# Float64 weights to float32: the low word rounded to three bits and added as an integer, with a shorter schedule of steps

## Chip, cores and metric

One core of one Trainium2 chip. The metric is device time in microseconds from start to end of one execution; it is the median over several runs. Profiles come from one further execution, which the hardware profiler recorded.

## What is computed

Three layers follow one another: an attention with 32 global and 512 local tokens per sequence (4 sequences, 8 heads of 64), where a local token sees the global ones and a window of 32 to either side; an FFN with squared ReLU; and an FFN whose activation is a rational function.

```python
a_l = sm(concat(s_lg, where(|i - j| <= 32, s_ll, -1e9)));  out_l = a_l @ concat(v_g, v_l)
x = attn_out.transpose(0, 2, 1, 3).reshape(2176, 512)
h = x @ w_in;   x = (max(h, 0) ** 2) @ w_out                   # moe:  512 -> 2048 -> 512
h = x @ w_in2;  P = a0 + a1*h + a2*h*h + a3*h*h*h              # moe2: 512 -> 2048 -> 512
Q = 1 + |b0|*|h| + |b1|*h*h;  out = (P / (Q + 1e-6)) @ w_out2
```

The FFNs' weights reach the chip as float64 (pairs of 32-bit words, the low word first), or as float32 where the host gives them so; here they are float64.

## The kernel before

**Products.** TensorE multiplies in a 32-bit format with a shortened significand (float32r). Each factor is split in a high and a low part, and a product is three matmuls (high by high, low by high, high by low). The hidden dimension of 2048 is cut in 16 chunks f of 128. The tokens are cut in groups of 384 or 256, six for each FFN. `step(k)` handles chunk f of one group: `do_h` (12 matmuls, L250), `relu2` in the first FFN (L263 on ScalarE, squares at L267 and L269, the low part at L274 on VectorE) or `rat_a` to `rat_c` in the second, and `do_y`, the second product (L326, L329), for a chunk two or three steps back. `x_split` (L234, L235) makes the parts of the next group's input.

**Weights.** An item is half a chunk: 128 columns of `w_in` or 128 rows of `w_out`, 128x512 elements. An item that comes as float64 (mode "wide") takes these steps: `w_load` (DMA of 512 KB to a buffer S, of which there are three), `w_abs` (L120, ScalarE: absolute value of the high words into a buffer T, of which there are four), `w_clamp` (L123: range of the exponent), `w_shift` (L127) and `w_sign` (L131), which make the float32 word that the high word gives, `w_pow` (L135) and `w_rest` (L139), which turn the low word into a float32 number of the right size, and `w_add` (L142, GpSimd), which adds it. Then `w_hi` (L151, ScalarE) rounds T to the high part, or, for an item that is needed later, a DMA writes T to DRAM (L147), and `w_lo` (L157, GpSimd) subtracts the high part. An item that waits in DRAM is loaded from there (L110) as float32 and takes only `w_hi` and `w_lo`. Wide items are 64: chunks 0 to 6 of the first FFN, then its chunks 14 and 15 (to DRAM), its chunks 7 to 13, and all 32 halves of the second FFN (to DRAM).

**What sets the order.** Every engine runs its instructions in the order in which the kernel's code writes them. `cv_tick` advances the conversion by one step; a new item begins every three steps. A table gives the step of its life in which an item comes to each operation: OE for the 21 items that begin in the attention (there GpSimd clamps, "eclamp"), OL for the 43 wide ones that begin in the FFNs (VectorE clamps), OS for items that are float32 already. Within a step, ORD is the order. The attention calls `cv_tick` once or twice for each of its 40 groups of queries; `step(k)` calls it five, five and four times in turn for the first FFN's first group of tokens, then three times every second chunk. All DMAs are issued on SP's queue, in program order, and wait there for their buffers.

Of the kernel before, what the change touches and what calls it, by code (L numbers as in the profile page):

```python
# [18 lines left out]
EXP_MIN = 2.0 ** -15                     # as a word, 0x38000000: exponent 896 of a float64  # L19
EXP_MAX = 65536.0 * (2.0 - 2.0 ** -3 - 2.0 ** -23)  # as a word, 0x47efffff: the end of exponent 1150  # L20
# [3 lines left out]
def kernel(  # L24
# [49 lines left out]
    # Weights come as float64 (in 64-bit words) or float32.  Each f-chunk of 128 columns of  # L74
    # w_in and rows of w_out becomes float32 and then a pair of float32r parts.
# [4 lines left out]
    # three buffers that serve the attention first and the FFNs then  # L80
# [5 lines left out]
    def w_src(ap, ph, half, f, m):  # L86
        """DMA (destination rows, source) pairs; m words per element."""
        if half:
            return [(slice(0, 128), ap[f * 128:(f + 1) * 128, :])]
        c = ap[:, f * 128 * m:(f + 1) * 128 * m]  # L90
        if ph:
            return [(slice(0, 128), c.rearrange("(k p) f -> p k f", p=128))]
        v = c.rearrange("(u h d) f -> u d h f", u=2, d=D)
        return [(slice(64 * u, 64 * u + 64), v[u]) for u in range(2)]

    def w_load(it):
        """Starts the load of half an f-chunk; the first stage of its conversion."""
# [18 lines left out]
    # float64 words to the nearest float32: the high word gives the sign, the exponent and  # L116
    # 21 bits of the significand, the low word, scaled by that exponent, the rest.
# [4 lines left out]
    def w_clamp(it):  # L122
        (gp if "eclamp" in it["at"] else ve).tensor_scalar(it["T"], it["T"], EXP_MIN, EXP_MAX, ALU.max, ALU.min)  # L123

# [9 lines left out]
    def w_pow(it):  # L134
        ve.tensor_scalar(it["S"][:, :, 1], it["T"].bitcast(U32), 0xFF800000, None, ALU.bitwise_and)  # L135

    def w_rest(it):
        n = it["S"][:, :, 1].bitcast(F32)
        ve.scalar_tensor_tensor(out=n, in0=it["S"][:, :, 0], scalar=2.0 ** -52, in1=n, op0=ALU.mult, op1=ALU.mult)  # L139

    def w_add(it):
        gp.tensor_tensor(out=it["T"], in0=it["T"], in1=it["S"][:, :, 1].bitcast(F32), op=ALU.add)  # L142
# [19 lines left out]
    todo, line, cv = [], [], dict(z=0, early=False)  # L162
# [4 lines left out]
    # some chunks of the first pair and all of the second wait in DRAM as float32  # L167
# [12 lines left out]
    OPS = dict(hi=w_hi, pow=w_pow, clamp=w_clamp, rest=w_rest, lo=w_lo, add=w_add, shift=w_shift, sign=w_sign, abs=w_abs)  # L180
    # the step of its life in which an item comes to each operation: during the attention
    # (where GpSimd clamps), during the FFNs, and for an item that is float32 already
    OE = dict(abs=2, eclamp=3, shift=5, sign=5, pow=7, rest=7, add=7, hi=9, lo=12)
    OL = dict(abs=2, clamp=4, shift=5, sign=5, pow=7, rest=7, add=7, hi=9, lo=12)
    OS = dict(hi=5, lo=8)
    ORD = ("pow", "hi", "shift", "rest", "sign", "add", "clamp", "lo", "abs", "eclamp")

    def cv_tick(left):
        """One step of the conversion, which starts an item every three."""
# [8 lines left out]
        for nm in ORD:  # L198
            for it in line:
                if it["at"].get(nm) == it["age"]:  # L200
                    OPS[nm.replace("ecl", "cl")](it)
# [5 lines left out]
    # ------------------------------------------------------------ the two FFNs  # L207
    # x's parts, a ring of five pairs; the hidden chunk's parts and a scratch row, two sets
# [69 lines left out]
    # The rational function in three stages, each a chunk behind the one before: numerator and  # L278
    # denominator; a seed 1/Q = exp(-ln Q) and one Newton step on the quotient; the two parts.
# [32 lines left out]
    def do_y(j):  # L312
# [7 lines left out]
        # the products with hi first: lo comes after it  # L320
# [10 lines left out]
        def evac():  # L331
# [3 lines left out]
            else:  # L335
                for m in range(n // 128):
                    # the group's input is spent and its place holds the output
# [16 lines left out]
    def step(k):  # L354
# [15 lines left out]
        # the products of a chunk follow two or three chunks behind; one sooner where the  # L370
        # next group's input is being split
# [21 lines left out]
        # weights: the rest of the first pair, then the second, at most as far as slots are free  # L393
# [8 lines left out]
        # the hidden chunk's place is free only when the products before have read it  # L402
# [7 lines left out]
    # ------------------------------------------------------------ attention  # L410
    with ExitStack() as at:
# [10 lines left out]
        # raw queries and keys of the second quad, where a chunk of weights comes later  # L422
# [11 lines left out]
        # values by window, each head's with a column of ones behind, for the sums of a softmax  # L434
# [36 lines left out]
        # the global queries and keys pass through the space of two weight chunks  # L471
# [15 lines left out]
        # products that nobody reads bring the tensor engine to speed  # L487
# [8 lines left out]
        # masks: columns of a window are four blocks of 32 keys  # L496
# [29 lines left out]
        def prep_g(i):  # L526
            """All the global queries or keys, transposed."""
# [15 lines left out]
        def prep(n, i):  # L543
            """Transposes of one half of a quad's queries or keys."""
# [281 lines left out]
```

## Time and profile before

| | us |
|---|---|
| median of 3 runs | 986.23 |
| lowest and highest run | 984.02 and 991.07 |
| span of the profiled execution | 979.5 |
| TensorE busy | 922.1 |
| VectorE busy | 790.1 |
| ScalarE busy | 550.0 |
| GpSimd busy | 440.2 |

The span runs from the first to the last instruction of the profiled execution; the time of a run also has what lies around the program. PE is TensorE, PEld its loading of weights, DVE is VectorE, ACT ScalarE, POOL GpSimd, SP the engine that only issues DMAs; a q behind a name is that engine's sequencer. An idle time is put down to the engine and line that released the waiting instruction.

### The profile page before, as it was taken

Reading aid. Unit: us, or ns where it says so; the run is one execution under the profiler, and the core shown is the slowest. Engines: PE = TensorE matmul, PEld = TensorE weight load, DVE = VectorE, ACT = ScalarE, POOL = GpSimd, SP = SyncE. Lnnn points to the kernel's source line nnn. Section 1 sums busy time; section 2 is a strip of 40 time slices with the busy share of each in tenths; the row PEclk is TensorE's granted clock in tenths of the full one; section 3 lists DMA queues with packets and bytes.
Section 4 is the critical chain, followed back from the end, with each engine's and each line's share of the span. In section 5 each row is a group of like instructions: output and inputs, shape, how many; then the busy total and the mean of one; then the engine's idle time right before and its main releaser. Section 6 shows DMA issues by size and latency. Waiting matters only on the chain.

```text
span 979.5 us, 18271 instructions
## 1 busy us (share of the span) xinstructions
PE 922.1 (94%) x6794; PEld 835.7 (85%) x6794; DVE 790.1 (81%) x1599; ACT 550.0 (56%) x1180; POOL 440.2 (45%) x382
## 2 busy tenths in 40 slices
PE   8899988967999999999999988899999999999996
PEld 5676766957999999999999987688989989989875
DVE  5588889998865887567334589999999999999996
ACT  4697796544533443233233466566666666666764
POOL 2365565656211222111002468855555555555554
PEclk9999999989999999999999999999999999999999
DMA  9999996333533353332201322001010010010010
GB/s 225 200 225 236 222 195 165 102 105 108 148 120 97 97 161 99 97 97 76 65 1 44 95 68 67 31 1 33 1 33 1 1 33 1 1 33 1 1 33 22
DMA packets 78121, 81.82 MB, mean 84 GB/s; under 512 B 24528, under 2 KB 64720, under 8 KB 78032
## 3 DMA queue, kind: packets, MB, share of 16 engines
q1 hardware_dynamic: 78032, 80.66, 32.2%
q8 instruction: 53, 0.87, 0.4%
q14 instruction: 36, 0.29, 0.1%
HBM read 56.36 MB, written 13.89 MB: 72 GB/s over the span
## 4 chain that ended last, share of the span: by engine, by line
PE 63%; POOL 10%; DVE 9%; issue 6%; ACT 5%; DMA 5%; SPq 1%; POOLq 0%; DVEq 0%; ACTq 0%
PE S L250 29%; PE tr L326 6%; PE T L326 5%; PE PV L326 4%; PE PV L329 4%; PE tr L329 4%; PE T L329 4%; POOL w L157 4%; POOL T L142 2%; POOL big L306 2%; DMA S<-in_moe_w_in_dram 2%; DVE ts L298 2%; PE S L597 2%; DMA vw<-vw 1%; POOL tq L287 1%
## 5 line engine op out<-in xcount | busy, mean ns | idle before, releaser
L250 PE MATMUL S<-big,w 128*128 128x384 f32 (+1 forms) x2304 | 414.7, 329 | 1.6 <-POOL w L157 1.6
L250 PEld LDWEIGHTS S<-big,w 128*128 128x128 f32 x2304 | 390.2, 190 | 10.5 <-POOL w L157 1.9
L142 POOL TENSOR_TENSOR T<-T,S 128x512 f32<-128x512 f32 x64 | 87.6, 1369 | 244.4 <-DVE S L139 211.3
L287 POOL TENSOR_TENSOR tq<-tq,big 128x384 f32<-128x384 f32 (+1 forms) x96 | 93.5, 974 | 159.6 <-DVE tq L285 149.2
L271 DVE TENSOR_TENSOR big<-big 128x384 f32<-128x384 f32 (+1 forms) x80 | 56.5, 706 | 104.3 <-ACT big L267 104.2
L306 POOL TENSOR_TENSOR big<-ts,big 128x384 fp32r<-128x384 f32 (+1 forms) x96 | 124.3, 1295 | 5.2 <-issue 1.9
L298 DVE SCALAR_TENSOR_TENSOR ts<-ts,coef,big 128x384 f32<-128x384 f32 (+1 forms) x96 | 125.5, 1308 | 0.0
L157 POOL TENSOR_TENSOR w<-T,w 128x512 fp32r<-128x512 f32 x64 | 92.1, 1448 | 73.5 <-ACT w L151 72.0
L263 ACT ACTIVATE big<-S 128x384 f32<-128x384 f32 (+1 forms) x96 | 45.2, 471 | 125.1 <-PE S L250 120.3
L284 ACT ACTIVATE big<-S 128x384 f32<-128x384 f32 (+1 forms) x96 | 45.5, 474 | 105.1 <-PE S L250 77.3
L329 PE MATMUL PV<-w,big 128*128 128x512 f32 x288 | 100.0, 401 | 3.7 <-ACT big L305 2.6
L326 PE MATMUL T<-big,w 128*128 128x384 f32 x384 | 89.0, 340 | 14.8 <-DVE big L274 14.6
L329 PE MATMUL T<-w,big 128*128 128x512 f32 x288 | 84.2, 400 | 11.6 <-POOL big L306 10.9
L267 ACT ACTIVATE big<-big 128x384 fp32r<-128x384 f32 (+1 forms) x96 | 48.9, 509 | 62.2 <-PE T L326 26.5
L326 PEld LDWEIGHTS T<-big,w 128*128 128x128 f32 x384 | 69.0, 190 | 17.0 <-DVE big L274 17.0
L326 PE MATMUL PV<-big,w 128*128 128x384 f32 (+1 forms) x384 | 82.6, 323 | 0.0
L326 PE MATMUL tr<-big,w 128*128 128x384 f32 (+1 forms) x384 | 82.0, 322 | 0.0
L286 ACT ACTIVATE ts<-S,coef 128x384 f32<-128x384 f32 (+1 forms) x96 | 62.6, 652 | 25.9 <-POOL big L306 25.3
L274 DVE TENSOR_TENSOR big<-big,big 128x384 fp32r<-128x384 f32 (+1 forms) x96 | 68.3, 712 | 8.2 <-ACT big L269 2.4
L329 PEld LDWEIGHTS T<-w,big 128*128 128x128 f32 x288 | 52.0, 188 | 25.5 <-POOL big L306 17.6
L329 PE MATMUL tr<-w,big 128*128 128x512 f32 x240 | 71.5, 395 | 0.0
L120 ACT ACTIVATE T<-S 128x512 f32<-128x512 f32 x64 | 43.1, 673 | 49.5 <-DMA S<-in_moe_w_in_dram 29.9
(137 smaller groups left out, 1513.6 us busy)
## 6 DMA issues: line engine op xcount, KB each, us to landing
S<-in_moe_w_out_dram SPq DMA_DIRECT2D x32, 512.0 KB, 4.2
scr<-T SPq DMA_DIRECT2D x36, 256.0 KB, 4.4
T<-scr SPq DMA_DIRECT2D x36, 256.0 KB, 2.6
S<-in_moe_w_in_dram SPq DMA_DIRECT2D x32, 256.0 KB, 4.6
S<-in_moe_w_in_dram SPq DMA_DIRECT2D x16, 512.0 KB, 4.3
out_dram<-xT SPq DMA_DIRECT2D x17, 256.0 KB, 2.6
kr<-in_k_l_dram SPq DMA_DIRECT2D x7, 512.0 KB, 7.5
qr<-in_q_l_dram SPq DMA_DIRECT2D x7, 512.0 KB, 6.2
```

The lines of the kernel that those rows point to most:

```text
L142: gp.tensor_tensor(out=it["T"], in0=it["T"], in1=it["S"][:, :, 1].bitcast(F32), op=ALU.add)
L157: gp.tensor_tensor(out=w[:, 1, half], in0=it["T"], in1=w[:, 0, half].bitcast(F32), op=ALU.subtract)
L250: pe.matmul(h, wk[k][s], x[k][t], start=m == 0, stop=m == 3 * NK - 1)
L267: sc.activation(hi, g, AF.Square)
L271: ve.tensor_tensor(out=g, in0=g, in1=g, op=ALU.mult)
L274: ve.tensor_tensor(out=lo, in0=g, in1=hi.bitcast(F32), op=ALU.subtract)
L286: sc.activation(s, h, AF.Identity, scale=coef[:, 3:4], bias=coef[:, 2:3])
L287: gp.tensor_tensor(out=q, in0=q, in1=av, op=ALU.mult)
L298: ve.scalar_tensor_tensor(out=s, in0=s, scalar=coef[:, 0:1], in1=r, op0=ALU.add, op1=ALU.mult)
L306: gp.tensor_tensor(out=lo, in0=s, in1=hi.bitcast(F32), op=ALU.subtract)
L326: pe.matmul(y[m][:, 0:n], a, x, start=st and z == 0, stop=sp and z == 2)
L329: pe.matmul(y[m], a, x, start=st and z == 0, stop=sp and z == 2)
```

## The change

The low word is no longer turned into a float32 number. It is scaled by 2^-29 and written back as an integer, which rounds it to its upper three bits (0 to 8), in a step `w_low`. The word that `w_shift` and `w_sign` make has three free bits at its end, and `w_add` adds the two words as integers, on GpSimd as before. `w_pow` and `w_rest` fall away. `w_low` runs on GpSimd for the items that begin in the attention ("elow") and on ScalarE for the others; `w_clamp` is always on VectorE. The tables of steps are shorter: add at 6 or 5 instead of 7, and for the items in the FFNs `w_hi` at 7 instead of 9 and `w_lo` at 9 instead of 12. Comments go too, so lines shift by up to two.

```diff
     def w_clamp(it):
-        (gp if "eclamp" in it["at"] else ve).tensor_scalar(it["T"], it["T"], EXP_MIN, EXP_MAX, ALU.max, ALU.min)
+        ve.tensor_scalar(it["T"], it["T"], EXP_MIN, EXP_MAX, ALU.max, ALU.min)
+
+    def w_low(it):
+        u = it["S"][:, :, 0]
+        if "elow" in it["at"]:
+            gp.tensor_scalar(u, u, 2.0 ** -29, 0.0, ALU.mult, ALU.add)
+        else:
+            sc.activation(u, u, AF.Copy, scale=2.0 ** -29)
...
-    def w_pow(it):
-        ve.tensor_scalar(it["S"][:, :, 1], it["T"].bitcast(U32), 0xFF800000, None, ALU.bitwise_and)
-
-    def w_rest(it):
-        n = it["S"][:, :, 1].bitcast(F32)
-        ve.scalar_tensor_tensor(out=n, in0=it["S"][:, :, 0], scalar=2.0 ** -52, in1=n, op0=ALU.mult, op1=ALU.mult)
-
     def w_add(it):
-        gp.tensor_tensor(out=it["T"], in0=it["T"], in1=it["S"][:, :, 1].bitcast(F32), op=ALU.add)
+        u = it["T"].bitcast(U32)
+        gp.tensor_tensor(out=u, in0=u, in1=it["S"][:, :, 0], op=ALU.add)
...
-    OE = dict(abs=2, eclamp=3, shift=5, sign=5, pow=7, rest=7, add=7, hi=9, lo=12)
-    OL = dict(abs=2, clamp=4, shift=5, sign=5, pow=7, rest=7, add=7, hi=9, lo=12)
+    OE = dict(abs=2, elow=3, clamp=3, shift=4, sign=4, add=6, hi=9, lo=12)
+    OL = dict(abs=2, low=3, clamp=3, shift=4, sign=4, add=5, hi=7, lo=9)
     OS = dict(hi=5, lo=8)
-    ORD = ("pow", "hi", "shift", "rest", "sign", "add", "clamp", "lo", "abs", "eclamp")
+    ORD = ("hi", "add", "lo", "clamp", "shift", "sign", "low", "elow", "abs")
```

**VectorE in the first group of the first FFN, before.** One item and the beginning of the next; T and S are the buffers named above with the number of the tile, big1 and big2 hold the hidden chunk's parts.

```order
L274 TENSOR_TENSOR big1_2915<-big2_2916,big1_2915 128x384
L135 TENSOR_SCALAR S_3490<-T_3501 128x512
L139 SCALAR_TENSOR_TENSOR S_3490<-S_3490 128x512
L123 TENSOR_SCALAR T_3543<-T_3543 128x512
L127 TENSOR_SCALAR T_3543<-T_3543 128x512
L131 SCALAR_TENSOR_TENSOR T_3543<-S_3530,T_3543 128x512
```

The same place after; L124 is `w_clamp`, L135 `w_shift`, L139 `w_sign`, L276 what was L274.

```order
L139 SCALAR_TENSOR_TENSOR T_3519<-S_3508,T_3519 128x512
L124 TENSOR_SCALAR T_3561<-T_3561 128x512
L135 TENSOR_SCALAR T_3561<-T_3561 128x512
L139 SCALAR_TENSOR_TENSOR T_3561<-S_3521,T_3561 128x512
L276 TENSOR_TENSOR big1_2900<-big2_2901,big1_2900 128x384
L124 TENSOR_SCALAR T_3572<-T_3572 128x512
```

Before, five rows belong to an item (the two on S_3490 finish one item, the three on T_3543 begin the next); now three, and nothing on VectorE writes to S.

**GpSimd in the attention, before.** The clamp of one item, the add of the one before it, and the low part of a third; w2 and w3 are chunks of weights.

```order
L123 TENSOR_SCALAR T_1638<-T_1638 128x512
L142 TENSOR_TENSOR T_1504<-T_1504,S_1437 128x512
L157 TENSOR_TENSOR w3_1709<-T_1361,w3_1709 128x512
L123 TENSOR_SCALAR T_1797<-T_1797 128x512
L142 TENSOR_TENSOR T_1638<-T_1638,S_1565 128x512
L157 TENSOR_TENSOR w3_1709<-T_1504,w3_1709 128x512
```

The same place after; L144 is `w_add`, L159 `w_lo`, L129 the new `w_low`.

```order
L144 TENSOR_TENSOR T_1632<-T_1632,S_1560 128x512
L159 TENSOR_TENSOR w3_1703<-T_1357,w3_1703 128x512
L129 TENSOR_SCALAR S_1701<-S_1701 128x512
L144 TENSOR_TENSOR T_1790<-T_1790,S_1701 128x512
L159 TENSOR_TENSOR w3_1703<-T_1499,w3_1703 128x512
L129 TENSOR_SCALAR S_1854<-S_1854 128x512
```

In the place of the clamp on T stands the scaling of S, right ahead of the add of the same item and behind the low part of an earlier one.

**ScalarE in the first group of the first FFN, before.** L120 is `w_abs`, L151 `w_hi`, L263 to L269 belong to `relu2`.

```order
L120 ACTIVATE T_3543<-S_3530 128x512
L151 CAST w11_3532<-T_3488 128x512
L263 ACTIVATE big2_2916<-S_3551 128x384
L267 ACTIVATE big1_2915<-big2_2916 128x384
L269 ACTIVATE big2_2916<-big2_2916 128x384
L120 ACTIVATE T_3585<-S_3545 128x512
L151 CAST w12_3589<-T_3501 128x512
```

The same place after; L121 is `w_abs`, L131 the new `w_low`, L153 `w_hi`, L265 to L271 `relu2`.

```order
L121 ACTIVATE T_3519<-S_3508 128x512
L131 ACTIVATE S_3508<-S_3508 128x512
L265 ACTIVATE big2_2901<-S_3528 128x384
L153 CAST w12_3554<-T_3479 128x512
L269 ACTIVATE big1_2900<-big2_2901 128x384
L271 ACTIVATE big2_2901<-big2_2901 128x384
L121 ACTIVATE T_3561<-S_3521 128x512
```

Behind each `w_abs` now stands the scaling of the same item's low word.

## Rows read from the trace of the kernel before

**Rows 1.** The page, part 1: busy time, share of the span and instructions of each engine.

```profile
PE 922.1 (94%) x6794; PEld 835.7 (85%) x6794; DVE 790.1 (81%) x1599; ACT 550.0 (56%) x1180; POOL 440.2 (45%) x382
```

**Rows 2.** Windows by stage; columns in the first row: busy us (instructions), granted clock, DMA.

```profile
core 0: us, PE busy (x) PEld busy (x) DVE busy (x) ACT busy (x) POOL busy (x), PEclk, DMA share, GB/s
20.00:154.06 134.06, 119.61 (x2127) 92.23 (x2131) 106.64 (x444) 104.14 (x287) 69.44 (x47) 0.99 1.00 218
154.06:178.27 24.21, 21.79 (x349) 18.96 (x338) 21.23 (x71) 15.93 (x38) 13.92 (x8) 1.00 0.46 129
178.27:236.74 58.47, 45.51 (x226) 44.17 (x224) 57.09 (x67) 27.52 (x52) 34.73 (x25) 0.88 0.36 98
236.74:262.25 25.51, 22.14 (x122) 20.91 (x120) 20.19 (x29) 13.75 (x27) 14.08 (x10) 1.00 0.51 151
262.25:473.00 210.75, 210.75 (x1339) 210.75 (x1340) 146.48 (x276) 77.04 (x160) 38.55 (x28) 1.00 0.36 104
```

**Rows 3.** Groups by form, 178.27 to 236.74 us: busy us, mean ns, idle before <-releaser.

```profile
L326 PE MATMUL T<-big,w 128*128 128x384 f32 x58 | 14.4, 360 | 13.0 <-DVE big L274 13.0
...
L142 POOL TENSOR_TENSOR T<-T,S 128x512 f32<-128x512 f32 x13 | 18.6, 1427 | 25.9 <-DVE S L139 25.9
...
L157 POOL TENSOR_TENSOR w<-T,w 128x512 fp32r<-128x512 f32 x12 | 18.2, 1517 | 0.0
...
L131 DVE SCALAR_TENSOR_TENSOR T<-S,T 128x512 uint32<-128x512 uint32 x12 | 18.0, 1502 | 0.4
...
L127 DVE TENSOR_SCALAR T<-T 128x512 uint32<-128x512 uint32 x12 | 16.1, 1344 | 0.3
```

**Rows 4.** Timeline of one item, VectorE and GpSimd: start us, duration us.

```profile
207.61 0.42 DVE L123 TENSOR_SCALAR T<-T 128x512 f32<-128x512 f32 x1
...
207.78 1.43 POOL L142 TENSOR_TENSOR T<-T,S 128x512 f32<-128x512 f32 x1 [2.16 <-DVE S L139]
...
208.06 1.42 DVE L127 TENSOR_SCALAR T<-T 128x512 uint32<-128x512 uint32 x1
...
209.17 1.47 POOL L157 TENSOR_TENSOR w<-T,w 128x512 fp32r<-128x512 f32 x1
...
209.52 1.66 DVE L131 SCALAR_TENSOR_TENSOR T<-S,T 128x512 uint32<-128x512 uint32 x1
...
211.22 0.43 DVE L135 TENSOR_SCALAR S<-T 128x512 uint32<-128x512 uint32 x1
...
211.68 0.69 DVE L139 SCALAR_TENSOR_TENSOR S<-S 128x512 f32<-128x512 uint32 x1
...
212.45 1.39 POOL L142 TENSOR_TENSOR T<-T,S 128x512 f32<-128x512 f32 x1 [1.81 <-DVE S L139]
```

**Rows 5.** Timeline of one load, SP's queue and ScalarE.

```profile
198.95 1.26 SPq L114 DMA_DIRECT2D S<-in_moe_w_in_dram  x2
...
204.05 0.69 ACT L120 ACTIVATE T<-S 128x512 f32<-128x512 f32 x1 [3.91 <-DMA S<-in_moe_w_in_dram]
```

**Rows 6.** The lines L142 and L123 on GpSimd: ns min/median/max.

```profile
L142 POOL TENSOR_TENSOR T<-T,S x64: 1282/1377/1567, 41.4 to 473.1; 128x512 f32<-128x512 f32 x64
...
L123 POOL TENSOR_SCALAR T<-T x21: 1913/1915/2365, 27.8 to 174.2; 128x512 f32<-128x512 f32 x21
```

**Rows 7.** Chain of waits, 78 to 92 us: start us, duration us.

```profile
83.26 0.77 DVE S L135
84.05 0.71 DVE S L139
```

**Rows 8.** Timeline of GpSimd in the attention, two of its clamps.

```profile
44.81 1.91 POOL L123 TENSOR_SCALAR T<-T 128x512 f32<-128x512 f32 x1 [2.11 <-ACT T L120]
...
149.57 1.92 POOL L123 TENSOR_SCALAR T<-T 128x512 f32<-128x512 f32 x1 [0.77 <-ACT T L120]
```

More of the change, by code (lines that the diff above doesn't have):

```diff
@@ L161 @@
     done = set()
-    todo, line, cv = [], [], dict(z=0, early=False)
+    todo, line, cv = [], [], dict(z=0, early=True)
     def items(ph, fs, mode, spill=False):
@@ L178 @@
     todo.reverse()
-    OPS = dict(hi=w_hi, pow=w_pow, clamp=w_clamp, rest=w_rest, lo=w_lo, add=w_add, shift=w_shift, sign=w_sign, abs=w_abs)
-    OE = dict(abs=2, eclamp=3, shift=5, sign=5, pow=7, rest=7, add=7, hi=9, lo=12)
-    OL = dict(abs=2, clamp=4, shift=5, sign=5, pow=7, rest=7, add=7, hi=9, lo=12)
+    OPS = dict(hi=w_hi, abs=w_abs, clamp=w_clamp, low=w_low, shift=w_shift, sign=w_sign, add=w_add, lo=w_lo)
+    OE = dict(abs=2, elow=3, clamp=3, shift=4, sign=4, add=6, hi=9, lo=12)
+    OL = dict(abs=2, low=3, clamp=3, shift=4, sign=4, add=5, hi=7, lo=9)
     OS = dict(hi=5, lo=8)
-    ORD = ("pow", "hi", "shift", "rest", "sign", "add", "clamp", "lo", "abs", "eclamp")
+    ORD = ("hi", "add", "lo", "clamp", "shift", "sign", "low", "elow", "abs")
     def cv_tick(left):
@@ L200, in cv_tick @@
                 if it["at"].get(nm) == it["age"]:
-                    OPS[nm.replace("ecl", "cl")](it)
+                    OPS[nm.replace("el", "l")](it)
         line[:] = [it for it in line if it["age"] < it["at"]["lo"]]
@@ L727 @@
         cv["job"] = 0
-        cv["early"] = True
         LD = ("k", "A", "q", "B", "")
```

## Prediction

> **What bounds the kernel now.** The profiled execution took 979.5 us, and TensorE was busy for 922.1 us of it [rows 1]; the median of the runs shown is 986.2 us, 6.7 us more, so I make the sum against the span and add 6.7 us at the end. A share of 94% says little about a change in weight conversion. I therefore cut the span into stages with the windows view [rows 2], and the reader should compare TensorE's column with the length of each window.
>
> - 20 to 154 us, attention: TensorE is busy for 119.6 of 134 us, the DMA engines have a share of 1.00, and VectorE (106.6) and ScalarE (104.1) lie close behind. No engine alone is the bound.
> - 154 to 178 us, end of the attention: VectorE 21.2 of 24.2 us.
> - 178 to 237 us, the FFN's first group of tokens: TensorE 45.5 of 58.5 us at a granted clock of 0.88, VectorE 57.1 of 58.5.
> - 237 to 262 us: TensorE 22.1 of 25.5 us.
> - 262 to 473 us: TensorE 210.75 of 210.75 us. Conversion goes on here, wholly hidden.
>
> So conversion is paid for between 154 and 262 us, where TensorE idles for about 19 us. In the third stage the grouped rows show who waits [rows 3]: TensorE's 13.0 us of idle time before L326 end with L274 on VectorE, which stands in VectorE's queue behind conversion steps, and GpSimd's 25.9 us of idle time before L142 all end with L139 on VectorE. VectorE in turn is held by GpSimd. L127 lasts 1344 ns on average here and L131 1502 ns; in the timeline of one item [rows 4] L127 ends just after L142 does and L131 just after L157 does, while the same-shaped L123, which gets in just ahead of L142, takes 0.42 us. The two engines take turns: an item is L142 plus L157 (about 2.9 us) and then a stretch in which GpSimd waits for the rest of L131, L135 and L139 (212.45 less the end of L157 at 210.64: 1.81 us; 2.16 us on average, 25.9 / 12, with L274 in some of them). Twelve items from 178.27 to 236.74 make 4.87 us each.
>
> **The change, part by part.**
>
> *Two VectorE steps go, per item.* L135 and L139 disappear 64 times. In the third stage they are the very steps that end GpSimd's wait: from the start of L135 to the end of L139 are 1.15 us (211.22 to 212.37) [rows 4]. After the change the step before the add is w_sign (L139 in the new numbering), and the order listing shows three VectorE rows per item instead of five. Clamp still gets in ahead of the add, shift between the two GpSimd steps, and about 0.6 us of sign remain behind the last of them. The cycle becomes 4.87 - 1.15 = 3.72 us. I allow 0.15 us for the load: three buffers S mean that a load starts when the add three items back is done, and the one at 198.95 kept ScalarE waiting until 204.05, 5.1 us [rows 5]. In a cycle of 3.7 us that is just in time. Gain: 12 x 1.0 = 12 us. TensorE needs at most the 45.5 us that it was busy, so it doesn't stand in the way of 58.5 - 12 = 46.5 us; where it idles less, its clock of 0.88 can only recover.
>
> *The end of the attention.* Four items that go to DRAM, 24.2 us. Their clamp (L123) ran on GpSimd; now VectorE does it for 0.42 us, and GpSimd scales the low word in its place. VectorE saves 0.43 + 0.69 - 0.42 = 0.70 us per item [rows 4], 2.8 us; TensorE idles for only 2.4 us of this stage, and I take 2.
>
> *237 to 262 us.* VectorE's shorter queue brings L274 forward, and an item's buffers come free up to three steps sooner, so the float32 reloads stand less in the way on SP's queue. TensorE idles for 3.4 us here; I take 1.5.
>
> *Attention.* VectorE loses 17 x 0.70 = 12 us of its 106.6. On the chain of waits its conversion steps stand only where the engines catch up after a late transfer, as at 83.26 and 84.05 us [rows 7], and the DMA engines at share 1.00 don't get less to do. I take 3 us, between 0 and 12.
>
> *What is added to ScalarE.* 43 scaled copies of 128x512 (new L131). The nearest row is its strided read of the same words, 0.69 us [rows 5]. Between 178 and 237 us ScalarE is busy for 27.5 of 58.5 us [rows 2], and the copy is wanted only by the add, behind clamp, shift and sign. Hidden: 0. Without that cover it would be 12 x 0.69 = 8 us.
>
> *What is added to GpSimd.* 21 scalings of the low word (new L129) for 21 clamps, and 64 adds of integers instead of floats. No row shows GpSimd on integers. For the add I take the float row: 1.28 to 1.57 us, median 1.38 [rows 6]; the lower bound is 1.28, and as the upper one I take 1.92, that of the slowest operation of this tile on GpSimd. Each of 16 items would then cost 0.54 us more: 9 us. For the scaling I take the clamp's 1.92 us, also two scalar operations on 512 elements [rows 6]; the lower bound is 1.28 (an item at the end of the attention then gains 0.6 us, 2.6 us in all) and the upper one twice the clamp, 3.83, if the conversions in and out cost as much again (4 x 1.92 = 8 us more at the end of the attention). In the attention itself it is covered: clamps followed each other every 7.5 us (14 intervals from 44.81 to 149.57) [rows 8], and add, subtraction and scaling are 1.28 + 1.28 + 1.92 = 4.5 us.
>
> The Trainium skill's "GPSIMD Engine Reference", section "Engine selection", says that GpSimd runs operations of one input at roughly line rate, unlike those of two. By this the scaling would take, as an estimate from that page's 1.2 GHz, about 0.43 us plus overhead, and four items would give some 6 us more, still inside the forecast's own range. The trace disagrees: the clamp with its one input takes 1.92 us and the add with two 1.38, and the measurement decides.
>
> *SP's queue.* No DMA is added. The store of a finished item to DRAM now stands one load earlier, because its step is 7 and no longer 9; it waits for an add that VectorE and GpSimd were given two steps before, and these items run from about 240 us on, most of them under a TensorE that doesn't wait [rows 2]. Cost 0.
>
> Sum: 12 + 2 + 1.5 + 3 = 18.5 us. 979.5 - 18.5 = 961 us of span, and with 6.7 us around it 968 us as a time.
>
> **Rivals.**
>
> 1. *GpSimd is slower on integers, within the bounds above.* For it: all three operands' type is new to the trace, and the add sits in the cycle that takes turns. Against it: the same number of elements and of streams. The costs of both upper bounds are 9 + 8 = 17 us, of the add alone 9: 977 to 985, middle 979.
> 2. *GpSimd becomes the bound, and the kernel is slower.* One mechanism: the scaling of the low word at the attention's pace. Its place in the queue is behind add and subtraction, so the room for it is 7.5 - 2.6 = 4.9 us; from there on every further microsecond is paid 17 times in the attention, and at the end of it every one above 1.92 us four times. At three times the clamp's row (1.92 us, so 5.75) it is 17 x 0.85 + 4 x 3.83 = 30 us, so 968 + 30 = 998. It eats up the 18.5 us at 5.2 us. For it: conversions to and from integers are the one thing that no row prices. Against it: nothing in the trace of this engine on a 128x512 tile lasts more than 2.4 us.
> 3. *The load or ScalarE takes over as the cycle.* From an add to the next in the same buffer: 5.1 (load) + 0.69 + 0.42 + 0.42 + 0.69 + 1.38 = 8.7 us, a third of it 2.9 us per item, under 3.72. Only if each of the three VectorE steps is held once by a GpSimd operation (1.4 us) and ScalarE's copy falls into the loop (0.69), it is 13.6, or 4.5 us per item. That leaves 12 x 0.34 = 4 of the 12 us: 976.
> 4. *The attention gives way too.* VectorE is at 80% of it, and its steps are held less, since the burst of GpSimd's three operations now starts when its last step is done. If all 12 us come through instead of 3: 968 - 9 = 959.
>
> That the change doesn't do what it says is possible only as a part of 1: the VectorE steps do go, by the order listing.
>
> **How the numbers follow.** Chances: forecast 0.48 (its own range 961 to 974), rival 1 0.22, rival 2 0.12, rival 3 0.08, rival 4 0.10. A measurement of this kernel tells about 1% from no change: faster means under 976.4, slower above 996.1. Faster: the forecast and rival 4 (0.58), half of rival 3 (0.04) and, of rival 1, the part in which only a little is added (0.08): 0.70. Slower: rival 2, 0.12. Within 1%: the rest, 0.18. The range leaves out rival 2 (0.12) and the far ends of rivals 1 and 4 (0.07): 957 to 985.
>
> **What would show each step.** Right: between the end of the attention and the next group, adds on GpSimd follow each other by 3.6 to 3.9 us; GpSimd's idle time before them ends with the sign step and is about 1 us per item; the granted clock of this stage rises above 0.88; the first group ends about 15 us sooner counted from 154 us, while the stretch that was 262 to 473 us keeps its length. The new add has a row near 1.4 us, the new scaling near 1.9, ScalarE's copy near 0.7. Wrong: an add or a scaling on GpSimd of twice that; GpSimd without idle time in the attention; ScalarE's waits for S growing in the first group; or a cycle of 3.7 us with TensorE still waiting for L276, which would mean that another step in VectorE's queue holds it.

## The result, and the profile after

The changed kernel takes 972.6 us in the median of 4 runs (969.42 to 974.23); the kernel before, run beside it, 985.12 us (982.37 to 991.07). The ratio is 0.985, 95% interval 0.981 to 0.990: 12.5 us or 1.5% faster. The forecast was 968 us, with a range of 957 to 985, and faster as the likeliest case.

The page of the kernel after, part 1 (busy us, share of the span, instructions of each engine), answers to [rows 1]:

```profile
PE 922.0 (95%) x6794; PEld 833.5 (86%) x6794; DVE 725.4 (75%) x1492; ACT 573.1 (59%) x1223; POOL 411.9 (42%) x382
```

VectorE lost 65 us, GpSimd 28, ScalarE gained 23, and TensorE has the same work. The windows by stage answer to [rows 2]; the bounds lie near the same places of the program but not exactly on them, so lengths are compared by marks further down, and here the busy times and clocks are read (columns in the first row):

```profile
core 0: us, PE busy (x) PEld busy (x) DVE busy (x) ACT busy (x) POOL busy (x), PEclk, DMA share, GB/s
20.00:159.85 139.85, 125.00 (x2134) 95.79 (x2131) 96.97 (x439) 105.27 (x290) 49.51 (x47) 0.96 1.01 215
159.85:176.80 16.95, 16.59 (x319) 13.65 (x317) 14.20 (x58) 12.33 (x32) 6.31 (x6) 1.00 0.55 145
176.80:188.19 11.39, 11.18 (x66) 10.86 (x65) 5.63 (x12) 7.96 (x16) 4.74 (x4) 1.00 0.32 94
188.19:228.31 40.12, 34.69 (x193) 32.98 (x192) 39.05 (x38) 26.86 (x51) 30.24 (x22) 1.00 0.43 113
228.31:253.11 24.80, 21.31 (x119) 20.35 (x118) 16.41 (x24) 18.14 (x36) 14.31 (x11) 1.00 0.58 190
253.11:464.90 211.79, 211.79 (x1346) 211.79 (x1346) 115.61 (x217) 91.98 (x187) 38.46 (x29) 1.00 0.33 106
```

Up to the end of the attention VectorE and GpSimd are busy for less (97.0 and 49.5 us in the first row, before 106.6 and 69.4), and yet it does not end sooner. The granted clock in the stage of the first group is 1.00, before 0.88. In the last row TensorE never waits, as before; by the marks further down, from the twenty-first to the seventy-third hidden chunk, this stretch takes 195.0 us in both kernels.

The groups by form of the stretch 188.19 to 228.31 us answer to [rows 3] (busy us, mean ns of one, idle before and its releasers). L144 is the add, L159 the low part, L135 the shift, L139 the sign, L124 the clamp, L276 the step of the FFN that was L274:

```profile
L159 POOL TENSOR_TENSOR w<-T,w 128x512 fp32r<-128x512 f32 x11 | 16.6, 1509 | 0.0
L144 POOL TENSOR_TENSOR T<-T,S 128x512 uint32<-128x512 uint32 x11 | 15.6, 1416 | 12.0 <-ACT T L121 4.7 <-ACT big L265 2.9 <-issue 1.8
L135 DVE TENSOR_SCALAR T<-T 128x512 uint32<-128x512 uint32 x10 | 14.4, 1444 | 0.2
L328 PE MATMUL T<-big,w 128*128 128x384 f32 x48 | 11.5, 348 | 5.4 <-DVE big L276 5.3
...
L139 DVE SCALAR_TENSOR_TENSOR T<-S,T 128x512 uint32<-128x512 uint32 x10 | 10.8, 1080 | 0.3
...
L124 DVE TENSOR_SCALAR T<-T 128x512 f32<-128x512 f32 x10 | 8.0, 803 | 0.5 <-ACT T L121 0.5
```

GpSimd waits 12.0 / 11 = 1.1 us per add, before 25.9 / 13 = 2.0. (The prediction has 2.16: it divides by the twelve items of the stretch, but the 25.9 us also hold the wait before a thirteenth add, L142 x13 in [rows 3].) The stretch has ten items here and twelve in [rows 3], so TensorE's wait is compared over the whole first group, from the first to the seventeenth hidden chunk (bounds below), first before, then after:

```profile
L326 PE MATMUL T<-big,w 128*128 128x384 f32 x90 | 22.0, 354 | 14.6 <-DVE big L274 14.6
```

```profile
L328 PE MATMUL T<-big,w 128*128 128x384 f32 x90 | 21.4, 346 | 7.8 <-DVE big L276 7.7
```

TensorE's wait for L276 is down to 7.8 us from 14.6. The timeline of two items (start, duration, idle before), as [rows 4], shows why the cycle is now 3.5 or 4.1 us:

```profile
208.29 0.69 DVE L139 SCALAR_TENSOR_TENSOR T<-S,T 128x512 uint32<-128x512 uint32 x1
...
208.90 0.42 DVE L124 TENSOR_SCALAR T<-T 128x512 f32<-128x512 f32 x1
209.12 1.38 POOL L144 TENSOR_TENSOR T<-T,S 128x512 uint32<-128x512 uint32 x1 [1.14 <-ACT T L121]
209.36 1.42 DVE L135 TENSOR_SCALAR T<-T 128x512 uint32<-128x512 uint32 x1
...
210.46 1.45 POOL L159 TENSOR_TENSOR w<-T,w 128x512 fp32r<-128x512 f32 x1
...
210.82 1.64 DVE L139 SCALAR_TENSOR_TENSOR T<-S,T 128x512 uint32<-128x512 uint32 x1
212.38 0.55 DVE L276 TENSOR_TENSOR big<-big,big 128x384 fp32r<-128x384 f32 x1
212.59 1.51 POOL L144 TENSOR_TENSOR T<-T,S 128x512 uint32<-128x512 uint32 x1 [0.68 <-issue]
...
213.42 0.97 DVE L124 TENSOR_SCALAR T<-T 128x512 f32<-128x512 f32 x1 [0.49 <-ACT T L121]
...
214.42 1.40 DVE L135 TENSOR_SCALAR T<-T 128x512 uint32<-128x512 uint32 x1
215.85 0.69 DVE L139 SCALAR_TENSOR_TENSOR T<-S,T 128x512 uint32<-128x512 uint32 x1
...
216.68 1.35 POOL L144 TENSOR_TENSOR T<-T,S 128x512 uint32<-128x512 uint32 x1 [1.14 <-ACT T L121]
...
216.80 1.66 DVE L276 TENSOR_TENSOR big<-big,big 128x384 fp32r<-128x384 f32 x1
```

Each of GpSimd's two operations holds one VectorE step: the held step ends 0.3 to 0.6 us after the GpSimd operation does (the shift at 210.78, after the add's end at 210.50; the sign at 212.46, after 211.91). In the first item these are the shift (1.42) and the sign (1.64); the next add follows 212.59 - 209.12 = 3.47 us later. In the second the clamp takes the first place (0.97), the shift the second (1.40), and the sign (0.69) still has to run when GpSimd is done; the add comes 216.68 - 212.59 = 4.09 us later. L276 at 216.80 (1.66 us) takes such a place too. The releaser named behind L144's idle time, ScalarE at L121, is only the last event; the add at 209.12 started when the sign ahead of it was done (208.29 + 0.69 = 208.98).

To compare stages between kernels I take one instruction as a mark: where ScalarE takes up the first FFN's first hidden chunk, and the seventeenth, the first of the next group of tokens. Their rows in the timeline of before, and behind them those of after:

```profile
168.06 0.49 ACT L263 ACTIVATE big<-S 128x384 f32<-128x384 f32 x1 [1.30 <-PE S L250]
...
260.04 0.47 ACT L263 ACTIVATE big<-S 128x384 f32<-128x384 f32 x1
```

```profile
172.21 0.49 ACT L265 ACTIVATE big<-S 128x384 f32<-128x384 f32 x1 [1.72 <-PE S L252]
...
251.51 0.48 ACT L265 ACTIVATE big<-S 128x384 f32<-128x384 f32 x1
```

Before, the first group takes 260.04 - 168.06 = 92.0 us, after 251.51 - 172.21 = 79.3 us, 12.7 less; the attention ends 4.1 us later. Of the 12.7 us, 11.3 lie between the fifth and the thirteenth hidden chunk (57.0 and 45.7 us), in which both kernels have eleven adds. "Group" below is this difference, "first mark" its beginning, and "cycle" the mean distance of eleven adds on GpSimd inside it (4.90 before, 4.01 after).

### The profile page after: what moved, and what is told of

It is laid out like the page before. It is cut to its first block, busy times and chain, and to the rows that moved or that the text cites. A ratio compares the mean times of both kernels' runs of the same rounds, so it can differ in the third digit from the quotient of the medians.

```text
span 972.5 us, 18297 instructions
## 1 busy us (share of the span) xinstructions
PE 922.0 (95%) x6794; PEld 833.5 (86%) x6794; DVE 725.4 (75%) x1492; ACT 573.1 (59%) x1223; POOL 411.9 (42%) x382
## 4 chain that ended last, share of the span: by engine, by line
PE 60%; DVE 10%; POOL 9%; ACT 8%; DMA 7%; issue 4%; SPq 1%; POOLq 0%; DVEq 0%; ACTq 0%
PE S L252 27%; PE tr L328 6%; PE T L328 5%; PE PV L328 5%; POOL big L308 4%; PE T L331 3%; PE PV L331 3%; PE tr L331 3%; DMA S<-in_moe_w_in_dram 3%; POOL w L159 2%; POOL tq L289 2%; PE S L599 2%; DVE ts L300 2%; DMA S<-in_moe_w_out_dram 2%; ACT ts L288 1%
## 5 line engine op out<-in xcount | busy, mean ns | idle before, releaser
L252 PE MATMUL S<-big,w 128*128 128x384 f32 (+1 forms) x2304 | 410.3, 327 | 1.1 <-ACT big L265 1.1
L252 PEld LDWEIGHTS S<-big,w 128*128 128x128 f32 x2304 | 385.8, 188 | 10.0 <-ACT big L265 1.4
L144 POOL TENSOR_TENSOR T<-T,S 128x512 uint32<-128x512 uint32 x64 | 86.5, 1352 | 272.7 <-DVE T L139 165.6
L273 DVE TENSOR_TENSOR big<-big 128x384 f32<-128x384 f32 (+1 forms) x80 | 47.5, 594 | 136.6 <-ACT big L269 136.4
L159 POOL TENSOR_TENSOR w<-T,w 128x512 fp32r<-128x512 f32 x64 | 91.2, 1434 | 82.4 <-ACT w L153 81.1
L265 ACT ACTIVATE big<-S 128x384 f32<-128x384 f32 (+1 forms) x96 | 45.3, 471 | 113.6 <-PE S L252 113.1
L328 PE MATMUL T<-big,w 128*128 128x384 f32 x384 | 88.2, 338 | 7.8 <-DVE big L276 7.7
L269 ACT ACTIVATE big<-big 128x384 fp32r<-128x384 f32 (+1 forms) x96 | 48.8, 509 | 64.5 <-PE T L328 27.0
L328 PE MATMUL PV<-big,w 128*128 128x384 f32 (+1 forms) x384 | 82.3, 322 | 0.2 <-DVE xs L704 0.2
L328 PE MATMUL tr<-big,w 128*128 128x384 f32 (+1 forms) x384 | 82.0, 322 | 0.0
L276 DVE TENSOR_TENSOR big<-big,big 128x384 fp32r<-128x384 f32 (+1 forms) x96 | 68.7, 716 | 13.7 <-ACT big L271 8.2
L328 PEld LDWEIGHTS T<-big,w 128*128 128x128 f32 x384 | 68.1, 188 | 10.1 <-DVE big L276 10.1
L331 PEld LDWEIGHTS PV<-w,big 128*128 128x128 f32 x288 | 52.5, 188 | 19.8 <-POOL big L308 7.8
```

The lines of the kernel that those rows point to most:

```text
L144: gp.tensor_tensor(out=u, in0=u, in1=it["S"][:, :, 0], op=ALU.add)
L159: gp.tensor_tensor(out=w[:, 1, half], in0=it["T"], in1=w[:, 0, half].bitcast(F32), op=ALU.subtract)
L252: pe.matmul(h, wk[k][s], x[k][t], start=m == 0, stop=m == 3 * NK - 1)
L269: sc.activation(hi, g, AF.Square)
L273: ve.tensor_tensor(out=g, in0=g, in1=g, op=ALU.mult)
L276: ve.tensor_tensor(out=lo, in0=g, in1=hi.bitcast(F32), op=ALU.subtract)
```

## The experiments

My theory (theory 1 in the expectations) was the prediction's: the two VectorE steps that went out of the cycle in which VectorE and GpSimd take turns are the gain. The first rival was that the shorter schedule is. Later ones were that ScalarE's new copy limits the cycle, and, for the attention, that the DMA engines, VectorE or GpSimd do.

**Both kernels again**, unchanged, one run each.

> The kernel before, unchanged, for a second profile. In the first pair of profiles ScalarE took up the first hidden chunk of the first FFN at 168.1 us before and at 172.2 us after the change, and the first group of tokens (first to seventeenth hidden chunk) took 92.0 us before and 79.3 us after. If the attention's length only scatters from one execution to the next, by when its transfers land, this profile can lie anywhere between 167 and 174 us and the group stays at 91 to 93 us. If the change itself makes the attention 4 us longer, it comes out at 168 us again, within 1 us.

> The changed kernel, unchanged, for a second profile. Scatter: the first hidden chunk anywhere between 167 and 174 us. The change lengthens the attention: 172 us again, within 1 us. Either way the first group takes 78 to 81 us.

Before: 983.92 us, first mark 170.45, group 92.5, cycle 4.89. After: 977.03 us, 170.99, 79.1, 4.02. The group repeats within 0.5 us, the attention within 1 to 3 us; that speaks for scatter in the attention and not for a fixed 4 us. The group's gain over both pairs is (92.0 + 92.5 - 79.3 - 79.1) / 2 = 13.0 us.

**The new arithmetic on the old steps.**

```diff
-    OE = dict(abs=2, elow=3, clamp=3, shift=4, sign=4, add=6, hi=9, lo=12)
-    OL = dict(abs=2, low=3, clamp=3, shift=4, sign=4, add=5, hi=7, lo=9)
+    OE = dict(abs=2, elow=3, clamp=3, shift=5, sign=5, add=7, hi=9, lo=12)
+    OL = dict(abs=2, low=4, clamp=4, shift=5, sign=5, add=7, hi=9, lo=12)
```

> The changed arithmetic with the steps of the kernel before: shift and sign at 5, add at 7, in the FFNs clamp and low at 4, high part at 9, low part at 12. Theory 1, VectorE and GpSimd take turns and the two VectorE steps less are the gain: the first group keeps 78 to 82 us, its adds keep a distance of 4.0 us, and the time stays at 970 to 977 us. Theory 2, the gain comes from buffers that are freed sooner by the shorter schedule: the adds go back to 4.6 to 4.9 us, the group to 88 us or more, the time to 980 to 986 us.

970.9 us (968.34 to 977.31), ratio to before 0.982 (0.976 to 0.989); group 77.6, cycle 3.86. The whole gain is there without the shorter schedule. It also separates the clock: the granted clock over the whole group is 0.93 before, 1.00 after and 0.96 here, and the shortest of the three groups is the one at 0.96, so the rise of the clock is not what makes the group shorter.

**The old arithmetic on the short steps.** The kernel before with its clamp still on GpSimd in the attention, and

```diff
-    OE = dict(abs=2, eclamp=3, shift=5, sign=5, pow=7, rest=7, add=7, hi=9, lo=12)
-    OL = dict(abs=2, clamp=4, shift=5, sign=5, pow=7, rest=7, add=7, hi=9, lo=12)
+    OE = dict(abs=2, eclamp=3, shift=4, sign=4, pow=6, rest=6, add=6, hi=9, lo=12)
+    OL = dict(abs=2, clamp=3, shift=4, sign=4, pow=5, rest=5, add=5, hi=7, lo=9)
...
-    ORD = ("pow", "hi", "shift", "rest", "sign", "add", "clamp", "lo", "abs", "eclamp")
+    ORD = ("hi", "pow", "rest", "add", "lo", "clamp", "shift", "sign", "eclamp", "abs")
```

> The arithmetic of the kernel before (its two VectorE steps on the low word, its add of floats, its clamp on GpSimd in the attention) with the short schedule of the changed kernel. Theory 1, taking turns: the adds stay 4.7 to 5.0 us apart, the first group takes 90 to 93 us, the time is that of before within 0.5% (980 to 988 us). Theory 2, the schedule: adds 4.0 to 4.3 us apart, group 79 to 84 us, time 971 to 977 us.

1051.93 us (1044.67 to 1054.83), ratio 1.064 (1.057 to 1.071): slower by 66 us, which no theory had. The first mark is at 225.26 us, some 56 us late; the group takes 101.9 us and its cycle is 5.08, both above the range of theory 1 and far from that of theory 2. So the shorter schedule alone brings no gain in the group, though with the attention upset this is no clean test of theory 1. The waits between 40 and 225 us (waiting engine and line <- releaser: us in total, times, longest) are led by two that before hardly has: between 40 and 168 us its L142 waits 4.1 us for L139, and its L127 never for L123:

```profile
POOL T L142 <- DVE S L139: 99.2, 16, 8.0
DVE T L127 <- POOL T L123: 76.4, 18, 4.5
ACT s L611 <- DVE nmx L603: 33.3, 15, 4.9
```

The chain of waits of the same kernel (start, duration, what) shows what it consists of:

```profile
103.37 1.30 POOL T L142
104.66 1.23 POOL w L157
105.89 1.88 POOL T L123
107.77 6.56 issue
```

The clamp (L123) stands in GpSimd's queue behind an add and a low part, 1.30 + 1.23 + 1.88 = 4.4 us, and the shift that needs it (L127) is now only one step later on VectorE, so the attention's own VectorE work queues behind the shift. In before the shift came two steps after the clamp. The changed kernel has the clamp on VectorE, which takes out this wait, and the scaling that replaced it on GpSimd is wanted only by the add, three steps later. That this is what makes its short schedule harmless is argued; no run moved the clamp alone.

**The low word of the later items on VectorE, and on GpSimd.** One part of the change elsewhere; each tests the taking of turns against ScalarE as the bound.

```diff
         else:
-            sc.activation(u, u, AF.Copy, scale=2.0 ** -29)
+            ve.tensor_scalar(u, u, 2.0 ** -29, 0.0, ALU.mult, ALU.add)
```

> In the FFNs the low word is scaled on VectorE and no longer on ScalarE; nothing else differs from the changed kernel. Theory 1, VectorE and GpSimd take turns and VectorE's steps set the distance of the adds: one step more of 0.45 us or so on VectorE makes it 4.4 to 4.7 us instead of 4.0, the first group 83 to 87 us instead of 79, the time 977 to 981 us. Rival, ScalarE: in the changed kernel GpSimd's idle time before the add is put down to ScalarE's lines (abs, the scaled copy) rather than to VectorE; if ScalarE holds the cycle, taking 0.67 us per item from it makes the distance 3.3 to 3.7 us, the group 73 to 76 us, the time 966 to 970 us.

```diff
-    OL = dict(abs=2, low=3, clamp=3, shift=4, sign=4, add=5, hi=7, lo=9)
+    OL = dict(abs=2, elow=3, clamp=3, shift=4, sign=4, add=5, hi=7, lo=9)
```

> In the FFNs the low word is scaled on GpSimd, as in the attention (0.67 us there), and no longer on ScalarE. Taking turns: 0.67 us more on GpSimd per item, so the adds are 4.5 to 4.8 us apart, the first group takes 84 to 88 us, the time is 977 to 981 us. ScalarE holds the cycle: 3.3 to 3.8 us, 73 to 77 us, 966 to 971 us.

On VectorE: 976.9 us (10 runs, 974.59 to 985.13), 0.992 (0.988 to 0.995), group 83.0, cycle 4.38. On GpSimd: 976.05 us (5 runs, 975.97 to 980.45), 0.992 (0.989 to 0.995), group 82.0, cycle 4.38. Both take work off ScalarE and both lose some 4 us of after's gain (their intervals and after's just overlap), and the group is 2.7 to 3.7 us longer. Groups by form, 188 to 226 us, first of the variant on VectorE, then of that on GpSimd; L131 and L129 are the scaling:

```profile
L131 DVE TENSOR_SCALAR S<-S 128x512 uint32<-128x512 uint32 x9 | 13.8, 1529 | 0.0
L144 POOL TENSOR_TENSOR T<-T,S 128x512 uint32<-128x512 uint32 x9 | 13.0, 1445 | 13.2 <-DVE T L139 9.5 <-issue 3.8
```

```profile
L144 POOL TENSOR_TENSOR T<-T,S 128x512 uint32<-128x512 uint32 x9 | 12.6, 1396 | 5.3 <-DVE T L139 3.4 <-issue 1.6
...
L129 POOL TENSOR_SCALAR S<-S 128x512 uint32<-128x512 uint32 x9 | 7.5, 833 | 0.8
```

ScalarE is not the bound. A step more on VectorE is held (1529 ns) and lengthens GpSimd's wait for the sign from 1.1 to 13.2 / 9 = 1.5 us. A step more on GpSimd shortens that wait to 5.3 / 9 = 0.6 us but costs 0.83 us of its own. Either way the cycle is 0.37 us longer, a little less than forecast (0.4 to 0.8): an operation costs in this cycle whichever of the two engines has it.

**The low part of the first FFN's later items on VectorE**, so that GpSimd holds VectorE once per item and not twice.

```diff
-            gp.tensor_tensor(out=w[:, 1, half], in0=it["T"], in1=w[:, 0, half].bitcast(F32), op=ALU.subtract)
+            e = ve if ph == 0 and it["at"] is not OE else gp
+            e.tensor_tensor(out=w[:, 1, half], in0=it["T"], in1=w[:, 0, half].bitcast(F32), op=ALU.subtract)
```

> For the items of the first FFN that begin behind the attention, the low part (1.45 us on GpSimd) is computed on VectorE; all else as in the changed kernel. Taking turns: an item is then 1.4 us of GpSimd and about 2.3 us of VectorE (0.42 + 0.42 + 0.69 + about 0.75) instead of 2.9 and 1.5, so the adds are 3.2 to 3.7 us apart, the first group takes 71 to 76 us, the time is 964 to 970 us, less than both kernels. Rival, VectorE's queue itself is what TensorE waits for (the low part of the hidden chunk stands in it): a longer queue keeps the group at 79 us or more and the time at 972 us or more.

968.65 us (6 runs, 965.2 to 973.55), ratio 0.983 (0.980 to 0.986); group 73.8, cycle 3.70. Groups by form, 188 to 226 us (L160 is the low part, L329 and L277 what were L328 and L276):

```profile
L144 POOL TENSOR_TENSOR T<-T,S 128x512 uint32<-128x512 uint32 x10 | 15.3, 1527 | 18.8 <-DVE T L139 7.7 <-ACT T L121 5.5 <-DMA S<-in_moe_w_in_dram 2.2
L329 PE MATMUL T<-big,w 128*128 128x384 f32 x48 | 11.6, 349 | 3.3 <-DVE big L277 3.3
...
L160 DVE TENSOR_TENSOR w<-T,w 128x512 fp32r<-128x512 f32 x11 | 10.9, 992 | 0.3 <-ACT w L153 0.3
```

GpSimd now idles 1.9 us per add, and yet the cycle is shorter: the low part costs VectorE 0.99 us in place of 1.51 on GpSimd, and one held place is gone. TensorE's wait over the whole group is 3.3 us in place of 7.8. In the group it is 5.5 us better than after; the intervals of the two ratios overlap, so in the median this version is ahead of after by 4 us without being told apart from it.

**What holds the attention.** Three experiments, for the term of the sum that did not come. More transfers: ten further copies of 512 KB in DRAM, issued behind the loads of `w_out`.

```diff
             sy.dma_start(d if half else d.rearrange("p (k f) -> p k f", k=NK), src)
+            if half and cv["early"]:
+                sy.dma_start(junk[f], src)
```

> The changed kernel with ten more transfers in the attention: each load of w_out there is followed by a copy of the same 512 KB from DRAM to a place in DRAM that nobody reads. Theory, the DMA engines and the SP queue pace the attention: 5.2 MB more at about 215 GB/s make it 15 to 28 us longer (the first hidden chunk at 186 to 200 us instead of 171). Rival, the compute engines pace it and the transfers have room: at most 5 us longer.

Less VectorE:

```diff
-    OE = dict(abs=2, elow=3, clamp=3, shift=4, sign=4, add=6, hi=9, lo=12)
+    OE = dict(abs=2, elow=3, add=6, hi=9, lo=12)
```

> The changed kernel without clamp, shift and sign for the 21 items that begin in the attention (these weights are then not converted). 63 VectorE steps of 0.42 to 0.69 us are left out, 32 us of VectorE. Theory, the attention is paced by transfers and by TensorE with ScalarE: the first hidden chunk stays at 168 to 173 us. Rival, VectorE paces it: 150 to 163 us.

The scaling on ScalarE and not on GpSimd (`low=3` for `elow=3` in the same line):

> The changed kernel with the low word on ScalarE in the attention too (21 copies of 0.67 us less on GpSimd, as many more on ScalarE). Theory, the attention is paced by transfers with ScalarE and TensorE close behind: the first hidden chunk at 171 to 178 us, the time 973 to 980 us. Rival, GpSimd's operations hold VectorE in the attention: 160 to 168 us, the time 963 to 970 us.

The windows from 20 to 170 us, of before, of after, of the one with more transfers, and of the one without VectorE steps (columns as above):

```profile
20.00:170.00 150.00, 133.13 (x2410) 103.09 (x2411) 121.62 (x499) 115.32 (x315) 80.14 (x52) 0.99 0.95 208
```

```profile
20.00:170.00 150.00, 134.79 (x2381) 103.12 (x2378) 106.65 (x484) 114.00 (x315) 53.64 (x51) 0.97 0.99 210
```

```profile
20.00:170.00 150.00, 132.73 (x2343) 101.74 (x2342) 104.34 (x482) 112.31 (x311) 53.55 (x51) 0.97 1.03 244
```

```profile
20.00:170.00 150.00, 135.88 (x2415) 104.71 (x2411) 86.04 (x447) 115.87 (x320) 55.96 (x53) 0.97 0.98 218
```

With 5.2 MB more, 244 in place of 210 GB/s, the time is 974.32 us (one run) and the first mark 173.3. Without 20.6 us of VectorE's work (121.62 before, 106.65 after, 86.04 here) it is 979.08 us (one run), first mark 172.29. With 21 scalings moved from GpSimd to ScalarE it is 975.67 us (4 runs, 972.56 to 978.34; ratio 0.988, 0.985 to 0.992), first mark 173.28. After itself lies at 172.21 and 170.99. So neither the volume of the transfers, nor VectorE, nor GpSimd sets the length of the attention: each end lies within 3 us of after's. The 21 copies more on ScalarE (8 us more busy in this window) move it by 1 to 2 us, no more than the scatter. The change itself had already taken 121.62 - 106.65 = 15 us from VectorE and 26.5 from GpSimd here.

**A later start of the conversion steps in the attention**, on top of the low part on VectorE, so that ScalarE doesn't wait for a load with the attention's work behind it:

```diff
-    OE = dict(abs=2, elow=3, clamp=3, shift=4, sign=4, add=6, hi=9, lo=12)
+    OE = dict(abs=4, elow=5, clamp=5, shift=6, sign=6, add=8, hi=10, lo=12)
```

> Low part on VectorE as in lo_vector, and in the attention an item's steps are two ticks later (absolute value at 4, clamp and scaling at 5, shift and sign at 6, add at 8, high part at 10), so that its load has more time to land before ScalarE comes to it. In the six profiles with the changed kernel's attention the first hidden chunk comes at 170.3 to 173.3 us, and ScalarE waits there for 13 to 16 us, in its queue ahead of the attention's exponentials, for the loads of its first step. Theory, these waits set the attention's length, and not the volume of the transfers nor VectorE: the first hidden chunk at 157 to 166 us, the time 955 to 965 us. Rival, TensorE and the attention's own loads set it, and ScalarE only waits where it would have waited anyway: 168 to 173 us, the time 966 to 972 us.

969.09 us (6 runs, 963.46 to 973.03), ratio 0.981 (0.977 to 0.985). ScalarE's waits at L121 between 20 and 165 us, first with the low part on VectorE alone, then with the later start as well:

```profile
ACT T L121 <- DMA S<-in_moe_w_in_dram: 10.7, 5, 5.6
...
ACT T L121 <- DMA S<-in_moe_w_out_dram: 4.8, 3, 3.1
```

```profile
ACT T L121 <- DMA S<-in_moe_w_out_dram: 1.7, 1, 1.7
ACT T L121 <- DMA S<-in_moe_w_in_dram: 1.5, 1, 1.5
```

The wait went from 15.5 to 3.2 us and the first mark came to 166.79, 3.5 us sooner than with the low part on VectorE alone (170.31). That lies between the ranges of theory and rival; the time is in the rival's. The group took 77.3 us in place of 73.8: the items were less far ahead when the FFN began (seventeen adds fall into the group in place of sixteen), and the gain was given back. The time is the same.

## Why the prediction came out right

**Direction and range** held for the main reason that the prediction gave: the group is 13.0 us shorter, against 12 + 1.5 = 13.5 forecast. Of the sum's 18.5 us the medians show 12.5; what failed is the attention's part. The arithmetic alone makes the group shorter (old steps: 77.6 us, 970.9 us in all), and work put back into the cycle on either engine takes 3 to 4 us of it away again.

**The cycle** was forecast at 3.72 us plus 0.15 for the load, "by 3.6 to 3.9". It is 4.01. The wait ends with the sign and is 1.1 us per item, as forecast, but the subtraction of 1.15 us, read from one timeline, supposed that the two held places always go to shift and sign. In two of three items one goes to the clamp or to L276, and the sign runs free behind: 4.1 us, else 3.5. The group still gained nearly what was forecast, and TensorE's wait for L276 fell by 14.6 - 7.8 = 6.8 us over the whole group; the clock of the stage rose from 0.88 to 1.00, as the prediction allowed. The sign "the first group ends about 15 us sooner" did not come: its end was 8.5 us sooner in the first pair (260.04 and 251.51) and 12.8 in the second (262.90 and 250.12), since the attention gave nothing.

**The steps that failed** are "Attention ... I take 3 us" and "The end of the attention ... I take 2". Five profiles with after's attention steps have the first mark at 170.3 to 172.4 us, two of before at 168.1 and 170.5. That is no gain; it may be a loss of about 2 us, which two profiles of before don't settle. The second one rested on VectorE's 21.2 of 24.2 us, the first on 12 us less of VectorE's work, of which the DMA share of 1.00 was to leave 3. Neither was a bound: VectorE lost 15 us up to 170 us by the change and 20 more in an experiment, and the end came no sooner; 16% more bytes went through, and it came at most 3 us later. So rival 4 fell. What does set the attention's length stays open. The waits of ScalarE for loads are one part, worth 3.5 us in one profile. On the chain of waits the transfers inside SBUF also stand (vw<-vw has 5 and 9% of the chain from 20 to 170 us in the two profiles of after), but no run took them away, so that is only argued.

**The base** of 6.7 us around the span was mis-sized. The profiled execution of after took 974.23 us for a span of 972.5, that of before, run again, 983.92 for 982.1: 1.7 to 1.8 us lie around the span. The span of 979.5 us was then that of an execution of about 981.3 us, less than any of the runs shown, and 5 of the 6.7 us was the scatter between runs. Adding it all was right for a forecast of the median, but not for the reason given. By the profiled pairs the gain is 7.0 us (979.5 to 972.5) and 6.9 (983.92 to 977.03); the medians of the runs say 12.5, of which the interval leaves 10 to 19. The group's 13.0 us are there in both pairs and are lost again in different places. In the first pair the attention ends 4.1 us later; in the second it ends 0.5 us later, but TensorE needs 4.4 us more from the twenty-first to the ninety-seventh hidden chunk (301.3 us in place of 296.9), at a granted clock of 1.00 and without waiting. The change does not always bring this: the first profile of after has 296.9 us there, as both of before. Twelve profiles (all but that of the short steps) show either 296.5 to 296.9 us (eight) or 301.3 to 301.7 us (four, all with the new arithmetic); why stays open, and two profiles of before can't tell whether the change makes it likelier. In both pairs some 0.4 us go up to the twenty-first chunk and 1.0 us in the second FFN (394.8 us from its first to its last hidden chunk before, 395.8 and 395.9 after). As an estimate from these, 13.0 - 2 - 0.4 - 1.0 = 9.6 us; the rest of the medians' 12.5 is not accounted for.

**The unknown prices.** The add on integers takes 1.31 us, the scaling on GpSimd 0.67, ScalarE's copy 0.67 (ns min/median/max, and when, by the lines of after):

```profile
L129 POOL TENSOR_SCALAR S<-S x21: 639/669/854, 27.7 to 178.2; 128x512 uint32<-128x512 uint32 x21
```

```profile
L144 POOL TENSOR_TENSOR T<-T,S x64: 1279/1308/1745, 31.3 to 457.0; 128x512 uint32<-128x512 uint32 x64
```

```profile
L131 ACT ACTIVATE S<-S x43: 655/667/691, 186.8 to 450.6; 128x512 uint32<-128x512 uint32 x43
```

So rival 1 and rival 2 fell at their premise. The scaling was taken at the clamp's 1.92 us and is below the lower bound of 1.28 that I had drawn from other lines. That did not harm the sum, which had no gain or cost for the scaling. The Trainium skill's "GPSIMD Engine Reference", section "Engine selection", says that GpSimd runs operations of one input at roughly line rate, which the prediction's estimate puts at 0.43 us plus overhead. The scaling (0.67 us) is near that and the clamp of the same shape (1.92 us) is not; the two differ in their operations, in type (uint32, float32) and in that the scaling takes every second word, and no run tells which of these decides. Rival 3 fell with the scaling on VectorE and on GpSimd: less work on ScalarE made it slower.

**The rest.** The stretch in which TensorE never waits kept its length in the first pair (from the twenty-first to the ninety-seventh hidden chunk 296.9 us in both), and the store that moved on SP's queue cost nothing there. The second FFN became 1.0 us longer in both pairs; the prediction has no term for it, and no run looked for the cause.

## What to carry to other kernels

Where VectorE and GpSimd take turns, count operations of both together: a step taken away from either shortens the cycle (two VectorE steps of 1.15 us in one timeline gave 0.89 us), and a step moved from one to the other gives back only a part (0.31 us for the low part, 1.51 us on GpSimd). Price such a cycle from several items and not from one timeline, since which step is held changes from item to item. A busy share near 1 of an engine or of the DMA engines is no bound until adding to it costs or taking from it helps; and when a schedule is shortened, look first at the steps that wait for another engine's queue.

## What the runs showed of the hardware

- GpSimd takes 0.67 us to scale 128x512 integers by a constant (every second word) and 1.92 us for the clamp (maximum and minimum, float32) of the same shape. An addition of integers takes 1.31 us against 1.38 for floats (medians; 1.28 to 1.75 and 1.28 to 1.57).
- A VectorE step that starts under a GpSimd operation ends 0.3 to 0.6 us after that one: 0.42 becomes 1.42 us (L135), 0.69 becomes 1.64 (L139), 0.55 becomes 1.66 (L276). "GPSIMD Engine Reference" of the Trainium skill, section "Key points", says that GpSimd shares its SBUF interfaces with VectorE, and that VectorE instructions in a 2-port performance mode or with two SBUF inputs contend. The rows of L139 and L276 agree for two inputs and add the size: the whole rest of the other engine's operation, and then the step. L135 has one input and is held all the same; no view here shows the mode that it runs in.
- With a DMA share of 0.99 the DMA engines still took 16% more bytes in the same time (210 to 244 GB/s, share 1.03); the added bytes went from DRAM to DRAM.
- With the same work and a granted clock of 1.00, a stretch in which TensorE never waits took 296.5 to 296.9 us in eight profiles and 301.3 to 301.7 in four; what makes the difference is open.
